# Batch 1's attention in blocks of 64 queries of two heads, batch 0 masked by VectorE with scores on half of TensorE's rows

## The chip, the cores and the metric

One core of a Trainium2 chip. The metric is device time in microseconds. The kernel before ran three times: 541.24, 541.22 and 537.54 us, median 541.22. One further execution was profiled.

## What is computed

The reference takes q, k, v of 4 batches x 8 heads x 576 positions x 64. Heads 0 to 3 are local (a query sees itself and the 31 positions before it), heads 4 to 7 strided (it sees the positions before it of the same class modulo 32). Two blocks of matrix products follow on the 512 channels.

```python
scores = scale * np.matmul(q, k.transpose(0, 1, 3, 2))
mask_local = (rel >= 0) & (rel < stride)                       # stride = 32
mask_strided = (rel >= 0) & (pos[None, :] % stride == pos[:, None] % stride)
attn = softmax(np.where(masks, scores, -1e9)); x = attn @ v    # x: (4, 576, 512)
h = relu(x @ w_in); u, v = split(h); v_n = layernorm(v)
v_s = einsum('ts,bsd->btd', w_spatial, v_n) + b_spatial
x = (u * v_s) @ w_out
theta = x @ w_theta
y = einsum(w_tok_r, x * cos(theta)) + einsum(w_tok_i, x * sin(theta))
u = x + y; out = u + relu(u @ w_ch)
```

## The kernel before, in words

Matrix products are made of pairs of f16 numbers (a high and a low part), three passes each. The weights come as 64-bit floats and are turned into such pairs on the chip, block by block: one ScalarE step (L203), three VectorE steps (L204 to L206), then the high part on ScalarE (L119 for all weights) and the low part on GpSimd (L211). These conversions and the attention of the next batch are woven into the main products of the batch before. A list `conv` has a due time for each block, ATT_AT (L54) a start and a pace in us for each batch's attention, and `others()` (L778) emits whatever is due by a clock that counts matmul columns. Within that, a scheduler fixes the order of instructions on every engine before the program runs; the main path's VectorE, ScalarE and GpSimd operations have a higher priority (`Ahead`, L99; their line in the profile is L108).

The main path of a batch is: v products (L578, main_v), the norm, u and sp products, x products with w_out, th products, and from th by sine and cosine on ScalarE the tile zf, which goes through DMA transposes on SyncE's queue (L686); then y products on zf and c products (main_end). The attention of batch b+1 must be over before main_v(b+1).

Batches 0 and 1 (N32 = 2) do their attention in f32 (attention32, L408), batches 2 and 3 with f16 pairs (attention, L485). The heads are taken in four pairs hp: 0 and 1 local, 2 and 3 strided with the positions sorted by class. For batches 0 and 1, q holds two heads on the two halves of the 128 rows and k comes from memory with zeros: `kzl`, `kzs` have, for head j, the other head's rows zero, so that a matmul over all 128 rows gives one head's scores. A load of k is 608 KB for a local pair and 576 KB for a strided one; the very first pair's is cut in two pieces of 384 and 224 KB (L309). After q and k of a pair comes its v (L318), four or five windows of 128 keys.

A unit is two blocks of a pair (96 queries local, 126 strided, with windows of 128 keys) of both heads, four score blocks of 128 columns; there are 11 units. scores32 (L375) first puts the mask into PSUM by a bf16 matmul of an identity with maskb (L383), then adds four score matmuls (L388). softmax32 (L392) on VectorE takes the maximum of all four blocks (L395) and negates it (L403), and four exponentials on ScalarE (L405) read PSUM and add up the sums. In kind "d" of E_WAY (two units of batch 0) VectorE subtracts (L398), one exponential does all (L400) and VectorE adds up (L401). A step later softmax_div (L340) makes the reciprocals (L341, L342) and multiplies (L343) on VectorE, TensorE transposes (L445), ScalarE copies (L446). Another step later the probabilities are multiplied with v (L420), two heads on two column halves, and x_evac (L345) writes a high part on ScalarE (L355) and a low part on VectorE (L356). The PSUM tile "av" exists once; in batch 1 the transposes use it too.

Batches 2 and 3 load q, k and v through staging tiles qs, ks and vs of their own (L269, L283, L285), convert them (L287 to L290, L295, L296), and mask with a fused VectorE instruction (softmax_exp, L327; L332) that adds the mask, scales by -1/8 and keeps the minimum for each row. Their qT, kT and vT share two slots with q, k and v of batches 0 and 1.

Of the kernel before, what the change touches and what calls it, by code (L numbers as in the profile page):

```python
# [11 lines left out]
F16 = mybir.dt.float16  # L12
BF16 = mybir.dt.bfloat16
F32 = mybir.dt.float32
# [20 lines left out]
E_WAY = ('aaaadaaadaa', 'aaaaaaaaaaa')  # L35
# [4 lines left out]
E_KLO = 'v'  # L40
E_PN16 = 'vvvv'
# [12 lines left out]
ATT_AT = (None, (2.7, 4.0), (74.5, 4.4), (169.9, 4.6))  # L54
# [10 lines left out]
def kernel(  # L65
# [31 lines left out]
    NZ = 2 * S // P  # L97

# [170 lines left out]
    def load_v(b, hp):  # L269
        nb = 6 if hp < 2 else 5  # L270
        vs = att_p.tile([P, 6, 2, 64], F32, tag="vs", name="vs")
        nc.sync.dma_start(vs[:, 0:nb], vl_d[b, hp] if hp < 2 else vs_d[b, hp - 2])
        return vs, nb

    def prep_qk(b, hp, j, tiles):
        local = hp < 2
        nk = S + STRIDE if local else S
        if j == 0:
            qT = att_p.tile([P, 2, S], F16, tag="qT", name="qT", bufs=2)
            kT = att_p.tile([P, 2, 2, S + STRIDE], F16, tag="kT", name="kT", bufs=2)  # L280
# [4 lines left out]
        ks = att_p.tile([P, S + STRIDE], F32, tag="ks", name="ks")  # L285
# [6 lines left out]
    def prep_v(ld):  # L292
        vs, nb = ld
        vT = att_p.tile([P, 2, 6, 2, 64], F16, tag="vT", name="vT", bufs=2)
# [6 lines left out]

    def load32(b, hp):
        local = hp < 2
        nb = 6 if local else 5
        qv = att_p.tile([P, S], F32, tag="qT", name="q32", bufs=2)
        kv = att_p.tile([P, 2, S + STRIDE], F32, tag="kT", name="k32", bufs=2)
        ksrc = kzl[b, hp] if local else kzs[b, hp - 2]
        first = b == 0 and hp == 0
        cuts = (0, 2 * LQ, S) if first else (0, S)  # L309
        for i, (c0, c1) in enumerate(zip(cuts, cuts[1:])):  # L310
            nc.sync.dma_start(qv[:, c0:c1], qp[b, hp][:, c0:c1])
            k0, k1 = (c0 + STRIDE if i else 0, c1 + STRIDE) if local else (c0, c1)
            nc.sync.dma_start(kv[..., k0:k1], ksrc[..., k0:k1])
            if first and i == 0:
                nc.sync.dma_start(mask, mask_d)
                nc.scalar.activation(maskb, mask, AF.Copy)
        vv = att_p.tile([P, 6, 2, 64], F32, tag="vT", name="v32", bufs=2)
        nc.sync.dma_start(vv[:, 0:nb], vl_d[b, hp] if local else vs_d[b, hp - 2])  # L318
        return qv, kv, vv

# [3 lines left out]
    def mask_of(hp, blk):  # L324
        return (1 if blk == 0 else 0) if hp < 2 else (3 if blk == 4 else 2)

    def softmax_exp(u, sc, sm, st):  # L327
        local = units[u][0][0] < 2
        R = LQ if local else P
        for n, (hp, j, blk) in enumerate(blocks_of(u)):  # L330

            nc.vector.tensor_tensor_reduce(out=sm[0:R, n, :], in0=sc[n][0:R], in1=mask[0:R, mask_of(hp, blk), :],  # L332
                                           op0=ALU.add, op1=ALU.min, scale=-0.125, scalar=3e38,
                                           accum_out=st[0:R, 1, n:n + 1])
        for n in range(4):
            nc.scalar.activation(sm[0:R, n, :], sm[0:R, n, :], AF.Exp, bias=st[0:R, 1, n:n + 1],  # L336
                                 scale=-1.0, accum_out=st[0:R, 2, n:n + 1])
# [37 lines left out]
    def scores32(u, tabs, sc, apart):  # L375


        R = LQ if units[u][0][0] < 2 else P
        mi = [mask_of(*un) for un in units[u]]
        for j0, j1 in ((0, 1), (1, 2)) if apart else ((0, 2),):  # L380
            for i0, i1 in [(0, 2)] if mi[0] == mi[1] else [(0, 1), (1, 2)]:
                shape = [P, i1 - i0, j1 - j0, P]
                nc.tensor.matmul(sc[0:R, i0:i1, j0:j1], identb[:, 0:R],  # L383
                                 maskb[:, mi[i0], :].unsqueeze(1).unsqueeze(1).broadcast_to(shape),
                                 start=(i0 == 0), stop=False)
        for n, (hp, j, blk) in enumerate(blocks_of(u)):
            o = LQ * blk if hp < 2 else SOFF[blk]
            nc.tensor.matmul(sc[0:R, n // 2, j], tabs[hp][0][:, o:o + R], tabs[hp][1][:, j, o:o + P],  # L388
                             start=False, stop=(n == 3 or (apart and n == 2)))
        return R  # L390

    def softmax32(sc, sm, st, R, way):  # L392
        X = mybir.AxisListType.X
        mx = st[0:R, 0, :]
        nc.vector.tensor_reduce(out=mx.rearrange("p (i j) -> p i j", i=2), in_=sc[0:R], op=ALU.max, axis=X)  # L395
        smv = sm[0:R].rearrange("p (i j) k -> p i j k", i=2)
        if way == "d":
            nc.vector.tensor_tensor(smv, sc[0:R], mx.rearrange("p (i j) -> p i j", i=2).unsqueeze(3).broadcast_to(  # L398
                [R, 2, 2, P]), ALU.subtract)
            nc.scalar.activation(sm[0:R], sm[0:R], AF.Exp, scale=0.125)  # L400
# [493 lines left out]
```

## Time and profile before

| | us |
|---|---|
| three runs, median | 541.22 |
| profiled execution | 538.83 |
| its span, first to last instruction | 536.8 |
| PE busy | 485.4 (90%) |
| DVE busy | 366.2 (68%) |
| ACT busy | 306.9 (57%) |
| POOL busy | 96.1 (18%) |
| mean granted TensorE clock | 0.977 |

PE is TensorE's matmuls, PEld its weight loads, DVE VectorE, ACT ScalarE, POOL GpSimd, SPq SyncE's DMA queue. An f32 matmul has two records. Durations of neighbouring operations on one engine overlap a little, so an operation's cost in a full queue is the distance from its start to the next one's start.

### The profile page before, as it was taken

To read this page: it belongs to the slowest core of one execution; us is meant where nothing else is said; L and a number is where in the kernel's file an instruction comes from. 1 tells how busy PE (TensorE), PEld (TensorE's weight loads), DVE (VectorE), ACT (ScalarE), POOL (GpSimd) and SP (SyncE) were. 2 spreads that over 40 slices of the span, in tenths; PEclk is the share of its full clock that TensorE was granted. 3 is DMA by queue.
4 is the path that set the end of the run, shared out by engine and by line. 5 is a ranking of instruction groups with operands and counts; after the bars stand their busy time and mean duration, and the time that the engine had idled before them with its cause. 6 is when DMAs were issued, how large, how long until landed. Compare 5 with 4: busy or idle time off the path is not lost. (4 is left out here: it accounts for less than half of the span.)

```text
span 536.8 us, 10338 instructions
## 1 busy us (share of the span) xinstructions
PE 485.4 (90%) x4019; PEld 365.7 (68%) x4019; DVE 366.2 (68%) x817; ACT 306.9 (57%) x737; POOL 96.1 (18%) x72
## 2 busy tenths in 40 slices
PE   6777978777887998999899998999999999996996
PEld 6764556555653776777666876777747777774775
DVE  1788999999987998898558778874389121227212
ACT  1777787667798436777585457764582121158101
POOL 0021134543300542001000400010003300100110
PEclk9789999999898998999999999999999999998999
DMA  8666577454159514755529034522082020004402
GB/s 278 239 232 189 162 262 219 161 152 139 37 98 244 136 40 108 194 135 143 137 40 137 1 81 127 148 45 37 1 150 27 1 89 1 1 2 91 86 1 88
DMA packets 75861, 59.88 MB, mean 112 GB/s; under 512 B 59939, under 2 KB 60963, under 8 KB 75813
## 3 DMA queue, kind: packets, MB, share of 16 engines
q1 hardware_dynamic: 75812, 59.23, 42.2%
q8 instruction: 31, 0.51, 0.4%
q14 instruction: 18, 0.14, 0.1%
HBM read 40.08 MB, written 4.72 MB: 83 GB/s over the span
## 5 line engine op out<-in xcount | busy, mean ns | idle before, releaser
L517 PE MATMUL y<-wtok,zf 128*128 128x288 f16 x864 | 108.8, 288 | 4.1 <-DMA zf<-vn 4.1
L517 PEld LDWEIGHTS <-zf 128*128 128x128 f16 x864 | 84.6, 99 | 27.7 <-DMA zf<-vn 4.7
L517 PE MATMUL sp<-wsp,vn 128*128 128x288 f16 x384 | 50.8, 286 | 2.1 <-ACT vn L108 1.6
L517 PE MATMUL c<-x2h,wch 128*128 128x288 f16 x384 | 49.6, 289 | 1.6 <-ACT o L108 1.6
L517 PE MATMUL x<-zf,wout 128*128 128x288 f16 x384 | 49.7, 288 | 0.0
L517 PE MATMUL th<-x2h,wth 128*128 128x288 f16 x384 | 49.6, 290 | 0.0
L517 PE MATMUL u<-xT,win 128*128 128x288 f16 x384 | 49.5, 286 | 0.0
L517 PEld LDWEIGHTS <-vn 128*128 128x128 f16 x416 | 40.3, 98 | 12.3 <-ACT vn L108 1.8
L578 PE MATMUL v<-win,xT 128*128 128x512 f16 x192 | 44.9, 387 | 3.0 <-DVE xT L356 1.9
L108 POOL TENSOR_TENSOR x2h<-x2f,x2h 128x576 f16<-128x576 f32 x20 | 27.6, 1381 | 110.4 <-DVE x2h L108 42.5
L517 PEld LDWEIGHTS <-wch 128*128 128x128 f16 x384 | 37.8, 99 | 11.7 <-issue 2.0
L517 PEld LDWEIGHTS <-wth 128*128 128x128 f16 x384 | 38.1, 100 | 10.3 <-issue 0.2
L517 PEld LDWEIGHTS <-wout 128*128 128x128 f16 x384 | 37.2, 98 | 9.5
L517 PEld LDWEIGHTS <-win 128*128 128x128 f16 x384 | 37.2, 98 | 9.1
L336 ACT ACTIVATE sm<-sm,st 96x128 f32<-96x128 f32 (+1 forms) x88 | 34.2, 390 | 7.8 <-DVE st L332 7.7
L578 PEld LDWEIGHTS <-xT 128*128 128x128 f16 x192 | 18.8, 99 | 25.3 <-DVE xT L356 2.6
L108 ACT ACTIVATE x2h<-x2f 128x576 f16<-128x576 f32 x24 | 16.5, 686 | 30.4 <-DVE x2f L108 30.0
L108 DVE SCALAR_TENSOR_TENSOR x2f<-y,x2f 128x576 f32<-128x576 f32 x16 | 12.0, 752 | 28.5 <-PE y L517 28.5
L108 POOL TENSOR_TENSOR zf<-u,zf 128x576 f16<-128x576 f32 x8 | 10.3, 1287 | 106.5 <-ACT zf L108 106.5
L108 DVE TENSOR_TENSOR ta<-ta,x2f 128x1152 f32<-128x1152 f32 x16 | 21.5, 1352 | 8.9 <-ACT ta L108 8.9
L108 ACT ACTIVATE o<-c 128x576 f32<-128x576 f32 (+1 forms) x17 | 10.3, 613 | 30.3 <-PE c L517 30.0
L343 DVE TENSOR_TENSOR sm<-sm,st 96x512 f32<-96x512 f32 (+1 forms) x33 | 26.7, 809 | 0.8
(122 smaller groups left out, 890.2 us busy)
## 6 DMA issues: line engine op xcount, KB each, us to landing
qs<-in_qd_dram SPq DMA_DIRECT2D x16, 288.0 KB, 3.0
out_dram<-o SPq DMA_DIRECT2D x15, 288.0 KB, 2.1
x2f<-in_w_in_dram SPq DMA_DIRECT2D x8, 512.0 KB, 5.3
ks<-in_kl_dram SPq DMA_DIRECT2D x8, 304.0 KB, 3.1
k<-in_kzs_dram SPq DMA_DIRECT2D x4, 576.0 KB, 5.4
wstg<-in_w_tr_dram SPq DMA_DIRECT2D x4, 576.0 KB, 4.7
wstg<-in_w_ti_dram SPq DMA_DIRECT2D x4, 576.0 KB, 4.7
ks<-in_ks_dram SPq DMA_DIRECT2D x8, 288.0 KB, 3.2
```

The lines of the kernel that those rows point to most:

```text
L108: return f(*args, **kwargs)
L336: nc.scalar.activation(sm[0:R, n, :], sm[0:R, n, :], AF.Exp, bias=st[0:R, 1, n:n + 1], scale=-1.0, accum_out=st[0:R, 2, n:n + 1])
L343: N[eng].tensor_tensor(sm[0:R], sm[0:R], st[0:R, 3, :].unsqueeze(2).broadcast_to([R, 4, P]), ALU.mult)
L517: nc.tensor.matmul(ps, lhs, rhs, **kw)
L578: nc.tensor.matmul(ps, xh[:, xe, c, i * P:(i + 1) * P], win[:, we, c, DM:2 * DM], start=(c == 0 and n == 0), stop=(c == NC - 1 and n == 2))
```

## The change

Batch 0 (attention0): k is loaded without zeros, each head into its half of the rows, the first pair's k on ScalarE's queue. The four score matmuls of a unit use 64 rows each, head 0 the lower and head 1 the upper half, into different PSUM banks. There is no mask matmul; softmax_exp masks on VectorE as in batches 2 and 3, one instruction a block. One unit (number 8, kind "p") takes the maximum so, subtracts on GpSimd, uses one exponential and adds up on VectorE. The multiplication of softmax_div moves to GpSimd for all 11 units.

Batch 1 (attention1): 12 units. A local unit is three blocks of 64 queries with windows of 96 keys, a strided one four (or three) blocks of 54 queries with 54 keys. Head 0's scores go to PSUM partitions 0 to 63 and head 1's to 64 to 127, each by a matmul over 128 rows with 64 columns of q, so that a unit has 288 or 216 columns on 128 partitions. k's zeros are written once, at the start, by four memsets into kts, and only the nonzero halves are loaded. v is loaded in blocks that begin where the windows begin: 4 DMAs for a local pair, 13 for a strided one, from the same arrays as before. The mask is loaded again in six pieces, and maskb made from it, when batch 1 begins.

Memory: kts (two tiles) and areg are allocated once. v of batches 0 and 1 lies in areg in two regions; over the same columns lie vT of batches 2 and 3 and their staging tiles: vst on columns 1536 to 2303 and qst on 2304 to 2879, the second region of v being 1408 to 2815, while kst lies behind it. identb is made on VectorE instead of GpSimd. Batch 1's pace in ATT_AT goes from 4.0 to 3.85 us a step.

```diff
-E_WAY = ('aaaadaaadaa', 'aaaaaaaaaaa')
+E_SUM = 'aaaaaaaapaa'
+E_PN32 = 'gv'
-ATT_AT = (None, (2.7, 4.0), (74.5, 4.4), (169.9, 4.6))
+ATT_AT = (None, (2.7, 3.85), (74.5, 4.4), (169.9, 4.6))
+    LK, SB, NLB, NSB = 96, 54, 9, 11
...
-    maskb = const.tile([P, 4, P], BF16, name="maskb")
-    nc.gpsimd.tensor_copy(identb, ident)
+    maskb = const.tile([P, 4, LK], BF16, name="maskb")
+    kts = [const.tile([P, 2, S + STRIDE], F32, name=f"kt{i}") for i in range(2)]
+    areg = const.tile([P, 6 * S + STRIDE], F32, name="areg")
+    v32s = [areg[:, i * NSB * P:(i + 1) * NSB * P].rearrange("p (n j d) -> p n j d", n=NSB, j=2) for i in range(2)]
+    vts2 = [areg[:, i * 6 * P:(i + 1) * 6 * P].bitcast(F16).rearrange("p (e n j d) -> p e n j d", e=2, n=6, j=2)
+            for i in range(2)]
+    vst = areg[:, 12 * P:18 * P].rearrange("p (n j d) -> p n j d", n=6, j=2)
+    qst = areg[:, 18 * P:18 * P + S]
+    kst = areg[:, 18 * P + S:18 * P + 2 * S + STRIDE]
+    nc.vector.tensor_copy(identb, ident)
+    for t in kts:
+        nc.vector.memset(t[0:64, 1, :], 0.0)
+        nc.vector.memset(t[64:P, 0, :], 0.0)
...
-        vs = att_p.tile([P, 6, 2, 64], F32, tag="vs", name="vs")
+        vs = vst
...
-            kT = att_p.tile([P, 2, 2, S + STRIDE], F16, tag="kT", name="kT", bufs=2)
+            kT = kts[hp % 2].rearrange("p j n -> p (j n)").bitcast(F16).rearrange("p (e j n) -> p e j n", e=2, j=2)
...
-        qs = att_p.tile([P, S], F32, tag="qs", name="qs")
+        qs = qst
...
+    units32 = [(hp, list(range(3 * u, 3 * u + 3)), LK) for hp in range(2) for u in range(3)]
+    units32 += [(hp, list(range(4 * u, min(4 * u + 4, NSB))), SB) for hp in (2, 3) for u in range(3)]
...
+    def load_kq(qv, kv, b, hp, c0, c1, k0, k1, by=nc.sync):
+        nc.sync.dma_start(qv[:, c0:c1], qp[b, hp][:, c0:c1])
+        ksrc = kzl[b, hp] if hp < 2 else kzs[b, hp - 2]
+        for j in range(2):
+            by.dma_start(kv[64 * j:64 * j + 64, j, k0:k1], ksrc[64 * j:64 * j + 64, j, k0:k1])
...
+    def scores32(u, tab, sc):
...
+        for n0, n1 in zip(cut, cut[1:]):
...
+            nc.tensor.matmul(sc[:, n0:n1, :], identb, maskb[:, mi, 0:W].unsqueeze(1).broadcast_to([P, n1 - n0, W]),
+                             start=(n0 == 0), stop=False)
+        for n, t in enumerate(blks):
+            for j in range(2):
+                nc.tensor.matmul(sc[64 * j:64 * j + 64, n, :], qv[:, q_at(W, t):q_at(W, t) + 64],
+                                 kv[:, j, k_at(W, t):k_at(W, t) + W], start=False, stop=(n == nb - 1))
...
+    def softmax32(u, sc, sm, st):
+        nc.vector.tensor_reduce(out=st[:, 0, 0:nb], in_=sc, op=ALU.max, axis=mybir.AxisListType.X)
+        nc.vector.tensor_scalar(st[:, 1, 0:nb], st[:, 0, 0:nb], -0.125, None, op0=ALU.mult)
+        for n in range(nb):
+            nc.scalar.activation(sm[:, n, :], sc[:, n, :], AF.Exp, bias=st[:, 1, n:n + 1],
+                                 scale=0.125, accum_out=st[:, 2, n:n + 1])
...
+    def pv32(b, u, tab, pT):
...
+            for j in range(2):
+                nc.tensor.matmul(av[64 * j:64 * j + 64, o:o + R], tab[2][0:W, t, j, :],
+                                 pT[0:W, n, 64 * j + r0:64 * j + r0 + R], start=True, stop=True)
...
-    def softmax_exp(u, sc, sm, st):
+    def softmax_exp(u, sc, sm, st, way="a"):
...
+            if way == "p":
+                nc.vector.tensor_tensor_reduce(out=sm[0:R, n, :], in0=sc[n][0:R], in1=mask[0:R, mi, :],
+                                               op0=ALU.add, op1=ALU.max, scale=1.0, scalar=-3e38,
+                                               accum_out=st[0:R, 0, n:n + 1])
...
+        if way == "p":
+            nc.gpsimd.tensor_tensor(sm[0:R], sm[0:R], st[0:R, 0, :].unsqueeze(2).broadcast_to([R, 4, P]), ALU.subtract)
+            nc.scalar.activation(sm[0:R], sm[0:R], AF.Exp, scale=0.125)
+            nc.vector.tensor_reduce(out=st[0:R, 2, :], in_=sm[0:R], op=ALU.add, axis=mybir.AxisListType.X)
...
-                R = scores32(s, tabs, sc, b == 0)
...
+                scs = [two[:, n % 2, n // 2 * P:n // 2 * P + P] for n in range(4)]
...
+                for n, (hp, j, blk) in enumerate(blocks_of(s)):
+                    o = LQ * blk if local else SOFF[blk]
+                    h = slice(64 * j, 64 * j + 64)
+                    nc.tensor.matmul(scs[n][0:R], tabs[hp][0][h, o:o + R], tabs[hp][1][h, j, o:o + P],
+                                     start=True, stop=True)
...
-                softmax_div("v", sm, st, R, XS)
+                softmax_div(E_PN32[b], sm, st, R, XS)
...
-    atts = [(attention32 if b < N32 else attention)(b) for b in range(B)]
+    atts = [attention0(), attention1()] + [attention(b) for b in range(N32, B)]
```

## Rows read from the trace of the kernel before

**Rows 1.** Busy time of each engine in stretches of the span. The columns are the stretch in us, its length, then for PE, PEld, DVE, ACT and POOL the busy time in us with the number of instructions, the granted TensorE clock as a share of 2.4 GHz, the share of the DMA engines' time and GB/s.
```profile
14.00:55.00 41.00, 32.13 (x252) 24.30 (x252) 35.38 (x90) 30.16 (x110) 7.67 (x6) 0.88 0.67 220
55.00:150.00 95.00, 77.97 (x624) 57.50 (x622) 90.77 (x173) 71.14 (x184) 36.67 (x24) 0.98 0.52 162
...
175.00:537.00 362.00, 346.30 (x2981) 264.94 (x2978) 218.15 (x508) 180.52 (x398) 50.77 (x35) 0.99 0.33 76
```

**Rows 2.** What TensorE waited for between 55 and 165 us: engine, tile and line that waited, what released it, then the sum of the waits in us, their number and the longest.
```profile
PE av L445 <- DVE xT L356: 7.7, 5, 3.1
PE av L445 <- DVE sm L343: 5.9, 3, 2.5
```

**Rows 3.** The start: a k load of the first 20 us (count, size, time to landing), the busy times of 10 to 20 us (columns as in rows 1), then the timeline of VectorE and of TensorE: start and duration in us, engine, line, operation, output and inputs, shapes, count, and in brackets the idle time before it and what ended it.
```profile
k<-in_kzl_dram SPq DMA_DIRECT2D x1, 608.0 KB, 6.8
...
10.00:20.00 10.00, 5.57 (x33) 5.38 (x32) 5.07 (x16) 5.03 (x24) 1.15 (x1) 0.71 0.98 356
...
8.42 0.69 DVE L395 TENSOR_REDUCE st<-at 96x4 f32<-96x512 f32 x1 [6.54 <-PE at L388]
14.12 0.43 DVE L204 TENSOR_SCALAR x2h<-x2f 128x512 int32<-128x512 int32 x1 [5.02 <-DMA x2f<-in_w_in_dram]
...
6.03 0.59 PE L383 MATMUL at<-maskb,identb 128*96 128x128 bf16 x4 [1.75 <-ACT maskb L316]
```

**Rows 4.** The timeline of VectorE, columns as in the second part of rows 3: batch 0's softmax steps at 31 to 35 us, and the fused masking and minimum of batch 2 at 200 us.
```profile
31.53 0.15 DVE L403 TENSOR_SCALAR st<-st 128x4 f32<-128x4 f32 x1
31.60 0.15 DVE L341 TENSOR_SCALAR st<-st 96x4 f32<-96x4 f32 x1
...
33.29 0.68 DVE L343 TENSOR_TENSOR smx<-smx,st 96x512 f32<-96x512 f32 x1
33.89 0.68 DVE L395 TENSOR_REDUCE st<-at 128x4 f32<-128x512 f32 x1
34.49 0.34 DVE L356 TENSOR_TENSOR xT<-av,xT 128x192 f16<-128x192 f32 x1
34.76 0.26 DVE L403 TENSOR_SCALAR st<-st 128x4 f32<-128x4 f32 x1
...
200.48 0.28 DVE L332 CUSTOM_DVE_ANT_0 sm<-sc,mask 96x128 f32<-96x128 f32 x1
...
200.68 0.28 DVE L332 CUSTOM_DVE_ANT_0 sm<-sc,mask 96x128 f32<-96x128 f32 x1
```

**Rows 5.** The timelines of GpSimd and VectorE side by side, columns as before: first four VectorE operations of 14 to 55 us that began beside a GpSimd operation, with the first of these GpSimd operations, then three operations at 249 us.
```profile
29.30 1.15 POOL L211 TENSOR_TENSOR win<-x2h,win 128x512 f16<-128x512 f32 x1 [9.95 <-ACT win L119]
...
29.88 1.11 DVE L343 TENSOR_TENSOR smx<-smx,st 96x512 f32<-96x512 f32 x1
...
39.21 1.14 DVE L341 TENSOR_SCALAR st<-st 128x4 f32<-128x4 f32 x1
...
48.66 1.65 DVE L343 TENSOR_TENSOR smx<-smx,st 128x512 f32<-128x512 f32 x1
...
52.83 1.19 DVE L205 SCALAR_TENSOR_TENSOR x2h<-x2f,x2h 128x512 int32<-128x512 int32 x1 [0.98 <-ACT x2f L203]
...
249.52 1.28 POOL L108 TENSOR_TENSOR zf<-u,zf 128x576 f16<-128x576 f32 x1 [2.71 <-ACT zf L108]
...
249.60 0.28 DVE L332 CUSTOM_DVE_ANT_0 sm<-sc,mask 128x128 f32<-128x128 f32 x1
...
250.04 1.37 DVE L288 TENSOR_TENSOR qT<-qs,qT 64x576 f16<-64x576 f32 x1 [0.15 <-ACT qT L119]
```

**Rows 6.** The timeline of TensorE in batch 0's attention and at the first unit of batch 1.
```profile
16.64 1.96 PE L388 MATMUL at<-k,q 128*96 128x128 f32 x8
...
43.80 0.65 PE L420 MATMUL av<-smx,v 128*64 128x126 f32 x8 [0.69 <-ACT smx L446]
44.39 0.39 PE L578 MATMUL v<-win,xT 128*128 128x512 f16 x1
44.61 0.60 PE L445 MATMUL sc<-ident,smx 128*128 128x128 f32 x4
...
52.35 0.42 PE L383 MATMUL sc<-maskb,identb 128*96 128x256 bf16 x2
52.61 1.04 PE L388 MATMUL sc<-k,q 128*96 128x128 f32 x8
53.48 0.59 PE L578 MATMUL v<-win,xT 128*128 128x512 f16 x2
```

**Rows 7.** Batch 2's first q load on SyncE's queue, all its q loads as a group (count, size, median time to landing), the first DMA transposes of zf, and TensorE where batch 1's attention ends and batch 2's begins.
```profile
8.36 0.33 SPq L284 DMA_DIRECT2D qs<-in_qd_dram  x1
...
qs<-in_qd_dram SPq DMA_DIRECT2D x16, 288.0 KB, 3.0
...
154.54 6.43 SPq L686 DMA_TRANSPOSE zf<-vn  x4
...
157.04 0.61 PE L458 MATMUL sc<-kT,qT 128*96 128x128 f16 x8
...
158.41 0.64 PE L420 MATMUL av<-pT,v 128*64 128x126 f32 x8
...
173.38 22.22 PE L517 MATMUL y<-wtok,zf 128*128 128x288 f16 x180
195.44 0.61 PE L458 MATMUL sc<-kT,qT 128*96 128x128 f16 x8
```

More of the change, by code (lines that the diff above doesn't have):

```diff
@@ new lines, in load_kq, with load_v32 @@
+    def load_kq(qv, kv, b, hp, c0, c1, k0, k1, by=nc.sync):
[3 more added lines that the diff above has]
+            by.dma_start(kv[64 * j:64 * j + 64, j, k0:k1], ksrc[64 * j:64 * j + 64, j, k0:k1])
+    def load_v32(vv, b, hp):
+        if hp < 2:
+            src = vl_d[b, hp]
+            nc.sync.dma_start(vv[0:LK, 0:9:3], src[0:LK, 0:6:2])
+            nc.sync.dma_start(vv[0:64, 1:9:3], src[64:P, 0:6:2])
+            nc.sync.dma_start(vv[64:LK, 1:9:3], src[STRIDE:64, 1:6:2])
+            nc.sync.dma_start(vv[0:LK, 2:9:3], src[STRIDE:P, 1:6:2])
+            return
+        src = vs_d[b, hp - 2]
+        for t in range(NSB):
+            p, end = k_at(SB, t), k_at(SB, t) + SB
+            at = p
+            while at < end:
+                w = max(i for i in range(5) if SOFF[i] <= at)
+                w = next((i for i in range(5) if SOFF[i] <= at and SOFF[i] + P >= end), w)
+                n = min(end, SOFF[w] + P) - at
+                nc.sync.dma_start(vv[at - p:at - p + n, t], src[at - SOFF[w]:at - SOFF[w] + n, w])
+                at += n
@@ L312, in load32 @@
             k0, k1 = (c0 + STRIDE if i else 0, c1 + STRIDE) if local else (c0, c1)
[L313 to L318, printed above, removed]
-        return qv, kv, vv
+            load_kq(qv, kv, b, hp, c0, c1, k0, k1, nc.scalar if first else nc.sync)
@@ L373, in spans_of, with attention0 @@
         return spans
[L375 to L400, printed above, removed]
-            nc.vector.tensor_reduce(out=st[0:R, 2, :], in_=sm[0:R], op=ALU.add, axis=X)
-        else:
-            nc.vector.tensor_scalar(st[0:R, 1, :], mx, -0.125, None, op0=ALU.mult)
-            for n in range(4):
-                nc.scalar.activation(sm[0:R, n, :], sc[0:R, n // 2, n % 2, :], AF.Exp, bias=st[0:R, 1, n:n + 1],
-                                     scale=0.125, accum_out=st[0:R, 2, n:n + 1])
-    def attention32(b):
+    def attention0():
+        b = 0
         tabs = {0: load32(b, 0)}
@@ L417, in attention32 @@
                 av = pa("av")
-                for i, hp, blk, r0, rows, o, t0 in pv_blocks(s - 2):
+                for i, hp, blk, r0, R, o, t0 in pv_blocks(s - 2):
                     for j in range(2):
-                        nc.tensor.matmul(av[64 * j:64 * j + 64, o:o + rows], tabs[hp][2][:, blk, j, :],
-                                         pT[:, 2 * i + j, r0:r0 + rows], start=True, stop=True)
+                        nc.tensor.matmul(av[64 * j:64 * j + 64, o:o + R], tabs[hp][2][:, blk, j, :],
+                                         pT[:, 2 * i + j, r0:r0 + R], start=True, stop=True)
                 x_evac(xT[b % 2], spans_of(s - 2), av)
@@ L441, in attention32 @@
                 sm, pT, st, R = un[s - 1]
[L442 to L443 removed]
+                softmax_div(E_PN32[b], sm, st, R, XS)
+                pt = pa4("sc")
                 for n in range(4):
```

135 lines of the change are left out of this document (105 added, 30 removed).

## The prediction, made before the changed kernel was run

> **What bounds the kernel now.** I read the table of busy time by stage first. From 175 us on TensorE is busy for 346.3 of 362 us, so nothing that leaves TensorE's work there alone can gain much [rows 1]. What the change touches lies before that. In the stretch 14 to 55 us VectorE is busy 35.4 of 41 us, ScalarE 30.2, TensorE 32.1 at a granted clock of 0.88. From 55 to 150 us VectorE is busy 90.8 of 95 us and TensorE 78.0 [rows 1]. So I then asked who TensorE waits for between 55 and 165 us: the two longest sums are batch 1's transposes, waiting 7.7 us for the difference of L356 and 5.9 us for the normalization of L343, both on VectorE [rows 2]. VectorE is what sets the pace until batch 1's attention is over. Before 14 us it is the DMA: VectorE does one reduction at 8.42 us and then stands for 5.0 us for the first block of w_in, while the DMA engines are 98% busy in 10 to 20 us [rows 3].
>
> **The start.** Ahead of w_in in the queue stand the k loads of the first two head pairs, 608 KB each with their zeros [rows 3]. Without zeros half of the two, 608 KB, goes. At the 356 GB/s of that stretch [rows 3] they are 622,592 B / 356 GB/s = 1.7 us, by which w_in lands earlier: -1.7 us, from 0 (if something else stands in front of VectorE then) to -2.8 us (at the 220 GB/s of the next stretch, [rows 1]). The first matmul no longer waits 1.75 us for the mask's cast on ScalarE [rows 3]; but VectorE's next work behind unit 0 is w_in either way, so I give that nothing. The four new memsets of 608 columns are about 0.7 us each, by the 0.60 us of a reduction over 512 [rows 4], together 2.8 us; VectorE idles for 6.5 us before 8.42 [rows 3], which hides them. If half of that cover were gone they would still fit.
>
> **Batch 0 on VectorE.** Prices are from start to start, since the ends overlap: a reduction of 512 elements 0.60, a normalization 0.60, the small negation 0.07, the fused mask-add and minimum with its accumulator read 0.20 to 0.21 a block [rows 4]. Before: nine units of 0.60 + 0.07 + 0.60 = 11.4, and two of kind "d" with two reductions, a subtraction and a normalization, 4 x 0.60 = 2.4 each, 4.8: 16.2 us. After: ten units of 4 x 0.21 = 8.4 and one of kind "p" with 0.84 + 0.60 = 1.4: 9.8 us. That is -6.4 us.
>
> Against it stand 12 operations that move to GpSimd (11 normalizations, one subtraction). A GpSimd tensor_tensor over 512 elements takes 1.15 us [rows 5], and VectorE operations that begin beside one are held until it ends: at 29.88 a normalization takes 1.11 instead of 0.68 us, at 39.21 the small L341 1.14 instead of 0.15, at 48.66 a normalization 1.65, at 52.83 a conversion step of the same size 1.19 [rows 4, 5]. The excess is 0.43 + 0.99 + 0.97 + 0.51 = 2.9 us over the six GpSimd operations of 14 to 55 us [rows 1, 5], 0.48 each. The fused reduction, with one operand in PSUM, is not held: at 249.60 it takes its 0.28 us inside a GpSimd operation, and the next VectorE operation, with both operands in SBUF, takes 1.37 [rows 5]. So what can be hit in batch 0 are the steps of w_in's conversion, three a block, and the small L341. I take 12 x 0.48 = 5.8, less the 1.4 us of the two normalizations that are no longer there to be hit: +4.4. Net -2.0 us. Ends: -7.8 us if the new operations hold nobody, and 12 x 1.15 - 7.8 = +6.0 us if each holds VectorE for its whole length. I take the value from the six measured ones.
>
> The Trainium skill ("SBUF — State Buffer", section "Who interferes with whom") speaks against this move: the port pair that VectorE and GpSimd share is an exclusive lock for the whole instruction, and the later one waits. By that rule the upper end, +6.0 us, is as possible as the mean; the sum would be -0.4 instead of -8.4. The trace agrees with the mechanism, not with that size: 0.48 us per operation.
>
> **Batch 0 on TensorE.** The mask matmuls go (0.25 us a unit) and the 0.87 us of scores [rows 6] run on row halves, two heads side by side. Pairs on two column halves show what pairing is worth: eight fp32 probability matmuls of 126 columns take 0.59 us, 74 ns each, against 109 ns for 128 columns unpaired [rows 6]. Up to 11 x (0.25 + 0.28) = 5.8 us; since VectorE is the later one in that stage I count 0. If the pairing gives nothing, 0 too. A loss is possible by the clock (third rival).
>
> **Batch 1.** A unit's reduction and normalization fall from 512 to 288 elements (local) or 216 (strided). Between 192 elements at 0.27 us (L356) and 512 at 0.60 [rows 4], 288 are 0.37 and 216 are 0.29 us. Local: 6 x 2 x 0.23 = 2.8 us. Strided: five units of 1.20 against six of 0.59, 6.0 - 3.5 = 2.5. The twelfth unit brings some 0.3 us of small operations. So -5.0 us of VectorE; at VectorE's share of the stage (0.955) -4.7 us. Ends: -1 us (if the waits of rows 2 only change their releaser) and -5.3. ScalarE's exponentials become 40 narrower ones instead of 44; TensorE has more, shorter matmuls (80 probability ones for 44, paired as before); both have room, 71 and 78 of 95 us [rows 1]. I count 0.
>
> **SyncE.** V in blocks comes in 34 loads instead of 4, k in two pieces, the mask again in 6: some 40 more issues at 0.33 us (the q load of [rows 7]), 13 us of issuing spread over the 110 us in which batch 1 is loaded and worked on. The weights' loads queue behind them, and their conversion stands in VectorE's line anyway; I count 0, at worst +3 us if a quarter of it meets an idle VectorE.
>
> **Batch 2.** Its stages for q and v now overlay the v of batch 1's second and fourth head pair. Today the first q load goes at 8.36 us, long before use; after, they can only go when batch 1's last probability matmul is done, 158.41 us [rows 7]. Behind that: two q loads in turn through one buffer with their conversions. But the third unit's scores come only at 195.44 [rows 7], so there is room to catch up. I count 0; the other end is the second rival.
>
> **Sum.** -1.7 - 2.0 - 4.7 = -8.4 us, against the profiled execution's 538.83 us: 530.4. The middle of the three runs is 541.22, 0.4% above it; from that the same sum gives 532.8. I predict the middle, **531.6 us**, 540.0 - 8.4.
>
> **Rivals.** (A) GpSimd's lock gives batch 0's saving back: -1.7 + 6.0 - 4.7 = -0.4, **539.6 us**. For it: each normalization starts just behind VectorE's reciprocal, so VectorE's next operation meets it at its start, and nearly 1 of 1.15 us was seen twice [rows 5]. Against it: 44 of VectorE's operations then are of the kind that isn't held.
> (B) Slower: the late loads of batch 2. Place: SyncE's queue and TensorE's order around 155 us. The scores of batch 2's unit 0 stand at 157.04 in front of the tail of v(1); if they stay there, TensorE waits for two q loads of 3.0 us [rows 7] with some 1.4 us of conversion each (two steps of the 0.68 us of rows 4), 9 us. A load that waits in SyncE's queue also holds the transposes of zf behind it, which begin at 154.54 and which y at 173.38 needs [rows 7]: 4.5 us if they begin at 159. Together +13.5: -8.4 + 13.5 = +5.1, **545.1 us**. It decides from 8.4 us of hold on. Against it: batch 1 ends earlier, and the static order may move the scores.
> (C) TensorE's clock. With less to do it may be granted the lower level for all of batch 0: the eight records of a unit's scores took 1.96 us at 16.64 against 1.04 at 52.61 [rows 6], nearly the two to one of 1.2 and 2.4 GHz. Work of 32.1 x 0.88 = 28.2 us at full clock, less 2.8 (masks) and half of 11 x 0.87, is 20.6; at half clock 41.2 us, where the forecast leaves 41 - 3.7 = 37.3: +3.9, so -4.5, **535.5 us**. Against it: 0.88 is the mean now.
> The Trainium skill ("TensorEngine Tiling (Array Packing)", section "Key Properties") says a change of tiling mode drains the array; batch 0 would get 22 more. No drain shows at the column-half changes of today: one 512-column matmul between two such groups takes 0.22 us from start to start, its usual spacing [rows 6]. If each cost the 0.17 us by which that matmul's length exceeds its spacing, 3.7 us would be added to TensorE, and C would gain weight.
>
> **How the numbers follow.** Forecast 0.50, A 0.17, B 0.15, C 0.18. A measurement of this kernel tells about 1% (5.4 us) from no change. Below 535.8 lie nine tenths of the forecast, half of C and a little of A: faster 0.56. Above 546.6 lies about half of B and a little of the rest: slower 0.11. Same 0.33. The range from 525 to 543 us takes in the lower ends (-1.7 - 7.8 - 5.3 = -14.8, 525.2), A and C, and leaves out most of B; the forecast's own is 527 to 536.
>
> **What would show it.** Right: first conversion of w_in at about 12.4 us; batch 0's last L356 at 50 instead of 54; VectorE's busy time up to 150 us some 7 us lower although single L205, L206 and L341 last over 1 us beside GpSimd; the y matmuls of batch 0 at 165 instead of 173.4 us; from there on the same distance to the end. Wrong: VectorE as busy as before in 14 to 55 us (A), TensorE idle at batch 2's first scores or late zf transposes (B), a granted clock under 0.75 in 14 to 50 us with TensorE waited for (C), or a later stage that grows.

## The result and the profile after

The changed kernel is slower: 547.1 us median of four runs against 541.2, ratio 1.012 [1.009, 1.016]. The forecast was 531.6 and a range to 543; what came is near rival B's 545.1.

The busy times of the three stretches of [rows 1], in the changed kernel:

```profile
14.00:55.00 41.00, 36.52 (x262) 23.23 (x261) 27.74 (x116) 30.12 (x106) 17.64 (x16) 0.88 0.54 159
55.00:150.00 95.00, 77.85 (x748) 55.74 (x747) 89.06 (x174) 66.04 (x168) 38.64 (x25) 0.93 0.47 152
175.00:537.00 362.00, 344.81 (x2961) 263.28 (x2960) 221.33 (x525) 186.38 (x415) 49.03 (x35) 0.98 0.33 74
```

From 14 to 55 us VectorE is busy 7.6 us less, but this is hardly work saved: before 14 us it is busy 6.5 instead of 1.6 us (the memsets and the first maskings come earlier), and by 55 us it has done 16 instead of 21 steps of w_in's conversion. From 55 to 150 us it is busy 1.7 us less, and TensorE's granted clock is 0.93 where it was 0.98. Behind 175 us TensorE's busy time is 1.5 us lower in the same 362 us: an idle stretch is new there. TensorE's waits from 55 to 205 us, the counterpart of [rows 2], show where:

```profile
PE av L569 <- DVE sm L418: 10.2, 6, 3.0
PE sc L582 <- DVE st L446: 7.6, 1, 7.6
PE av L427 <- ACT pT L570: 2.4, 1, 2.4
...
PE av L569 <- DVE xT L475: 1.6, 2, 1.0
```

One wait of 7.6 us is new. TensorE's timeline has it inside y(0), the y products of batch 0 (batches count from 0; L582 are scores of batch 2, L458 before, and L446 their masking, L332 before):

```profile
173.19 13.40 PE L641 MATMUL y<-wtok,zf 128*128 128x288 f16 x108
186.43 0.61 PE L582 MATMUL sc<-kt,qT 128*96 128x128 f16 x8
186.88 5.55 PE L641 MATMUL y<-wtok,zf 128*128 128x288 f16 x44
200.07 1.01 PE L582 MATMUL sc<-kt,qT 128*96 128x128 f16 x8 [7.63 <-DVE st L446]
200.87 5.69 PE L641 MATMUL y<-wtok,zf 128*128 128x288 f16 x28
```

The reader is to see three things. y(0) starts at 173.19 us, where it started before (173.38, [rows 7]): the lead of 8 us isn't there. The first two units of batch 2, at 157 and 160 us before, now stand inside y(0). And the second unit's scores wait for the one PSUM buffer of scores, which the first unit's masking gives back; the 28 y products behind the wait then take 0.20 us each on average, against 0.127 (the granted clock is 0.50 from 201 to 205 us and 1.00 from 206.4 us on). VectorE's timeline says why the masking is late:

```profile
193.62 1.22 DVE L110 TENSOR_TENSOR vn<-vr,vn 128x1024 f16<-128x1024 f32 x1
194.76 2.34 DVE L218 TENSOR_SCALAR wx<-wstg 128x512 int32<-128x512 int32 x1
197.03 0.28 DVE L446 CUSTOM_DVE_ANT_0 sm<-sc,mask 96x128 f32<-96x128 f32 x1
...
197.23 1.55 DVE L219 SCALAR_TENSOR_TENSOR wx<-wstg,wx 128x512 int32<-128x512 int32 x1
198.71 0.28 DVE L446 CUSTOM_DVE_ANT_0 sm<-sc,mask 96x128 f32<-96x128 f32 x1
```

The scores are there at 187.0; VectorE's fixed order has their four maskings behind batch 1's norm (vn) and between the steps of a weight's conversion. Batch 2's q loads, the counterpart of 8.36 us in [rows 7], went only when batch 1's last PV (161.8 us; PV are the products of the probabilities with v) had freed their staging:

```profile
165.03 0.53 SPq L298 DMA_DIRECT2D areg<-in_qd_dram  x1
...
170.13 0.36 SPq L298 DMA_DIRECT2D areg<-in_qd_dram  x1
```

### The profile page after: what moved, and what is told of

It is laid out like the page before. It is cut to its first block, busy times and chain, and to the rows that moved or that the text cites. A ratio compares the mean times of both kernels' runs of the same rounds, so it can differ in the third digit from the quotient of the medians.

```text
span 546.2 us, 10748 instructions
## 1 busy us (share of the span) xinstructions
PE 490.7 (90%) x4136; PEld 360.3 (66%) x4136; DVE 366.6 (67%) x881; ACT 307.4 (56%) x738; POOL 107.5 (20%) x83
## 5 line engine op out<-in xcount | busy, mean ns | idle before, releaser
L641 PE MATMUL y<-wtok,zf 128*128 128x288 f16 x864 | 112.2, 293 | 3.9 <-DMA zf<-vn 3.9
L641 PEld LDWEIGHTS <-zf 128*128 128x128 f16 x864 | 85.9, 100 | 29.0 <-DMA zf<-vn 4.7
L641 PE MATMUL u<-xT,win 128*128 128x288 f16 x384 | 51.3, 289 | 3.7 <-ACT win L121 2.3
L110 POOL TENSOR_TENSOR x2h<-x2f,x2h 128x576 f16<-128x576 f32 x20 | 26.4, 1320 | 118.2 <-DVE x2h L110 54.5
L702 PE MATMUL v<-win,xT 128*128 128x512 f16 x192 | 46.6, 397 | 0.8 <-ACT xT L474 0.4
L110 DVE TENSOR_TENSOR u<-u,sp 128x576 f32<-128x576 f32 x16 | 12.0, 749 | 21.0 <-PE sp L641 20.8
```

Source lines behind the costliest of these rows:

```text
L110: return f(*args, **kwargs)
L641: nc.tensor.matmul(ps, lhs, rhs, **kw)
L702: nc.tensor.matmul(ps, xh[:, xe, c, i * P:(i + 1) * P], win[:, we, c, DM:2 * DM], start=(c == 0 and n == 0), stop=(c == NC - 1 and n == 2))
```

## The experiments

First all runs in one table: the ratio to the kernel before, with its interval, and from each profile the starts of u(0), th(0), y(0) and th(1). From th(1) to the last matmul all 20 kernels take 265 to 270 us, so most of a difference is there at th(1). Each row is one profiled execution, and some lie a few us from their kernel's median: that of the kernel before 2.4 us below it, b0's 3.1 above, c1's 1.7 below.

| | ratio [95%] | u(0) | th(0) | y(0) | th(1) | y(0) to th(1) |
|---|---|---|---|---|---|---|
| before | 1 | 63.0 | 134.6 | 173.4 | 264.9 | 91.5 |
| after | 1.012 [1.009, 1.016] | 58.6 | 129.9 | 173.2 | 273.7 | 100.5 |
| e1_q_early | 1.007 [1.003, 1.010] | 63.0 | 133.5 | 177.1 | 275.5 | 98.4 |
| e2_before_overlay | 1.008 [1.005, 1.011] | 62.2 | 130.0 | 171.7 | 270.1 | 98.4 |
| e3_start_late | 0.999 [0.996, 1.002] | 58.4 | 130.4 | 174.3 | 269.1 | 94.8 |
| e4_norm_vector | 1.004 [1.001, 1.008] | 66.0 | 136.8 | 170.0 | 270.0 | 100.0 |
| b0_batch0_only | 0.998 [0.995, 1.000] | 60.2 | 126.7 | 168.1 | 267.2 | 99.1 |
| b1_batch1_only | 1.002 [0.999, 1.005] | 65.7 | 137.2 | 169.8 | 268.8 | 99.0 |
| c1_late_vv | 1.002 [0.999, 1.005] | 63.9 | 136.7 | 168.3 | 265.3 | 97.0 |
| e5_busy | 1.018 [1.015, 1.022] | 62.2 | 134.6 | 185.8 | 278.1 | 92.3 |
| e6_mask_ahead | 0.997 [0.994, 1.001] | 61.5 | 134.1 | 178.8 | 273.2 | 94.4 |
| b0_late | 0.996 [0.993, 1.000] | 61.5 | 128.0 | 168.0 | 264.2 | 96.2 |
| b0_ahead | 0.994 [0.991, 0.996] | 58.9 | 125.3 | 166.7 | 263.8 | 97.1 |
| e7_no_warm | 0.999 [0.997, 1.002] | 60.5 | 130.4 | 175.1 | 270.3 | 95.2 |
| e8_tight_ahead | 1.008 [1.004, 1.011] | 61.4 | 135.1 | 172.8 | 275.3 | 102.5 |
| e9_vv_ahead | 1.001 [0.999, 1.003] | 64.1 | 134.9 | 168.1 | 268.6 | 100.6 |
| e10_vv_tight_ahead | 1.001 [0.998, 1.004] | 65.4 | 138.7 | 171.9 | 269.3 | 97.4 |
| e11_vv_qearly_ahead | 1.008 [1.004, 1.011] | 67.6 | 138.0 | 181.1 | 273.3 | 92.2 |
| b0_units_first | 1.000 [0.997, 1.003] | 57.8 | 128.5 | 180.6 | 270.6 | 90.0 |
| full_units_first | 1.005 [1.002, 1.007] | 59.0 | 131.0 | 181.3 | 271.1 | 89.8 |

The profiled executions of e1 (548.6 us, median 543.2) and e6 (546.5, median 539.7) are the longest of their kernels; only waits, order and what the clock did are read from them.

**e1: q's staging moved to where it is free earlier.**

```diff
-    qst = areg[:, 18 * P:18 * P + S]      # over the v of batch 1's fourth head pair
+    qst = areg[:, 6 * P:6 * P + S]        # over that of the third; vst, vT and kst moved to fit
```

> The changed kernel with one thing moved: the buffer into which batch 2's q is loaded lies over the v of batch 1's third head pair, not of its fourth, so that q need not wait for batch 1's last PV (161.8 us). Theory (late staging: that wait makes batch 2's first masking late on VectorE, and TensorE stands 7.6 us in front of y(0)'s last passes, then 2.3 us at half clock): the wait for L446 at 192 to 200 us goes, y(0) ends near 201 instead of 211 us, and the time falls by 8 to 11 us, to 536 to 539 us, 2 to 5 us under the kernel before. Rival (the loss at y(0) comes from VectorE's order and GpSimd's holds, and q's load only happens to be late there): at most 2 us less, 545 to 547 us.

543.2 us, between the two. The first q load now goes at 136.52 us, but the second shares the staging buffer with it and waits for its conversion, and the wait in y(0) is still there:

```profile
136.52 0.33 SPq L298 DMA_DIRECT2D areg<-in_qd_dram  x1
...
163.40 0.43 SPq L298 DMA_DIRECT2D areg<-in_qd_dram  x1
```

```profile
PE sc L582 <- DVE st L446: 8.6, 1, 8.6
```

So an early first load alone does not bring the masking forward in VectorE's order. As the second load is still late, this run does not part the load from the order; e6 below does.

**e2: the overlay alone, on the kernel before.**

```diff
-        qs = att_p.tile([P, S], F32, tag="qs", name="qs")
+        qs = qst                              # over the second region of v of batches 0 and 1
```

> The kernel before with that one part of the change alone: q of batches 2 and 3 is staged over the v of the odd head pairs, which batch 1's last PV (158.4 us) still reads. Nothing else is changed. Late staging: the scores of batch 2's first unit (157 us before) stand in TensorE's order or in VectorE's behind a load that can't start before 159 us; 5 to 10 us more, 546 to 551 us. Rival (batch 2 has room to catch up, as the prediction had it): within 1.5 us of 541.2.

545.6 us, +0.8%, just under the lower end expected. The same wait appears in a kernel that has nothing else of the change:

```profile
PE sc L463 <- DVE st L337: 9.3, 1, 9.3
```

The overlay is thus enough to make the wait; room to catch up there was not.

**e3 and e6: the order alone.** e3 changes due times, e6 VectorE's priorities; buffers and loads stay.

```diff
-ATT_AT = (None, (2.7, 3.85), (74.5, 4.4), (169.9, 4.6))
+ATT_AT = (None, (2.7, 3.85), (86.0, 4.0), (169.9, 4.6))     # e3
```

```diff
+        with tc.high_priority(6000 if u < 2 else 0):              # e6, in att_scores
             softmax_exp(u, [sc[:, n, :] for n in range(4)], sm, st)
```

> The changed kernel with its buffers as they are; only the due times in the plan change, so that batch 2's attention is put into the order 11.5 us later and then in steps of 4.0 instead of 4.4 us (to end at about the same place). Late staging, where what hurts is that TensorE's order has batch 2's second scores ahead of y(0)'s last passes: the scores move out of y(0), the 7.6 us wait goes, and the time falls by 6 to 10 us, to 537 to 541 us. Rival (the lost time is VectorE's own, batch 2's masking has to be done somewhere in this stretch): 545 to 549 us.

> The changed kernel with buffers, loads and due times as they are; batch 2's first two units only get a higher priority for their masking and exponentials, which puts the four maskings of the first unit on VectorE ahead of the last steps of batch 1's norm instead of behind them (some 7 us earlier). Theory (order: the second unit's scores stand in TensorE's order inside y(0), wait there for the one PSUM buffer of scores, which is free only after the first unit's masking, and VectorE's order has that behind batch 1's norm): the wait of 7.6 us goes or falls under 2, and the time by 6 to 9 us, to 538 to 541 us. Rival (the masking only looks late; moving it holds up the norm, and y(0) or c(0) waits for that instead): within 2 us of 547.

540.6 and 539.7 us: both fall as the order theory said, by 1.3 and 1.5% of the changed kernel (from the ratios). In e3 y(0) runs through, in e6 the second unit's scores wait 1.05 us:

```profile
174.32 24.43 PE L641 MATMUL y<-wtok,zf 128*128 128x288 f16 x198
198.58 0.61 PE L582 MATMUL sc<-kt,qT 128*96 128x128 f16 x8
```

```profile
192.03 0.61 PE L582 MATMUL sc<-kt,qT 128*96 128x128 f16 x8
192.48 4.57 PE L642 MATMUL y<-wtok,zf 128*128 128x288 f16 x36
198.10 0.61 PE L582 MATMUL sc<-kt,qT 128*96 128x128 f16 x8 [1.05 <-DVE st L446]
```

In e6 q still comes late and the buffers are the same. The wait at y(0) is a matter of VectorE's order, and it is worth some 7 us. That leaves the change at no difference from before, with 8 us of the forecast still missing.

**b0 and b1: each part alone on the kernel before.** b0 has batch 0's part, with batch 2's staging its own; b1 batch 1's, with e3's late start.

```diff
-    atts = [(attention32 if b < N32 else attention)(b) for b in range(B)]
+    atts = [attention0(), attention32(1)] + [attention(b) for b in range(N32, B)]                        # b0
+    atts = [attention0(), attention1()] + ...      # b1: attention0 here is attention32(0) of before
```

> The kernel before with batch 0's part of the change alone: no mask added on TensorE, the fused masking on VectorE, k loaded and multiplied without zeros, the normalising on GpSimd. Batch 1 is masked on TensorE as before, and the staging buffers of batch 2 stay their own. By the prediction's terms (start -1.7, batch 0 -2.0): 537 to 538 us. Rival, TensorE's clock (seen in the first traces: with fewer matmuls in batch 0 the same 128x96 product takes 0.91 instead of 0.55 us for 10 to 20 us of the stretch from 20 to 42 us; before, for about 5 us): what VectorE gains goes there, 540 to 544 us.

> The kernel before with batch 1's part alone (12 units of 64 queries of two heads, normalised on VectorE), batch 0 as before. Its staging overlays are those of the changed kernel, but batch 2's attention is put into the order late, as in e3, so that the wait at y(0) is not there. By the prediction's term (-4.7 for batch 1): 536 to 537 us. Rival (a twelfth unit makes batch 1 end later, and TensorE's v(1) waits for it at 161 to 165 us, which eats VectorE's gain): 540 to 543 us.

Both rivals came closer than the forecast: 540.2 us (ratio 0.998) and 543.6 (1.002). But both reach y(0) early, by 5.3 and 3.5 us. b0 loses it by the same wait, although its staging is its own; b1 at the start of c(0), on ScalarE's conversion:

```profile
PE sc L524 <- DVE st L350: 8.7, 1, 8.7
```

```profile
PE c L680 <- ACT x2h L110: 5.1, 1, 5.1
```

So the overlay is one way into the wait, and a shift of the fixed order by batch 0's part is another.

**b0_late and b0_ahead: the wait taken from b0** by e3's due times and by e6's priority (diffs as there).

> b0 (batch 0's part alone on the kernel before, all staging buffers its own) with batch 2's attention put into the order late, as in e3. b0's trace reached y(0) at 168.1 us, 5.3 us earlier than the kernel before, and then waited 8.7 us there. If the gain is real and only the wait hides it: 531 to 534 us, faster than both kernels by 1.3 to 2%. Rival (as in b1 and c1, where TensorE did reach c(0) 5 us earlier and the time was still that of before: what comes late then, batch 2's attention, holds c(0) or x(1)): 539 to 542 us.

> b0 with the priority of e6 in place of the late start: the first unit's masking comes on VectorE some 5 us earlier, ahead of the vn steps but still behind the vr steps of batch 1's norm. By the order theory the 8.7 us wait falls to some 3 us: 534 to 536 us. Rival as for e6: 539 to 542 us.

539.3 us, the rival's, and 537.4, between the two. b0_ahead is faster than the kernel before by 0.4 to 0.9% and than the changed one by 1.8%, the best version found. Its wait is down from one of 8.7 us to three of together 3.0:

```profile
PE sc L524 <- DVE st L350: 3.0, 3, 2.0
```

Yet from its lead of 6.7 us at y(0) only 1.1 are left at th(1).

**e4, e5, e7: GpSimd's normalizing, TensorE's rate, the warm-up products.**

```diff
-E_PN32 = 'gv'
+E_PN32 = 'vv'                                 # e4
+                for _ in range(2):            # e5, on e3, ahead of batch 0's transposes
+                    nc.tensor.matmul(pt[:, 0, :], ident, ident, start=True, stop=True)
-WARM = 6
+WARM = 0                                      # e7, on e6
```

> The changed kernel with batch 0's probabilities normalised by VectorE instead of GpSimd (11 instructions of 512 elements, 1.04 us each on GpSimd, about 0.6 us on VectorE). If GpSimd's holds of VectorE cost what the prediction gave them (4.4 us) or more (its rival A): 2 to 5 us less, 542 to 545 us. If they lie beside other work, and the loss sits at y(0) alone: between 1 us less and 4 us more (546 to 551 us), since VectorE gets some 6 us of work back.

> e3 with two more matmuls of 128x128 fp32 (no part of the result) ahead of each of batch 0's 11 groups of transposes, where TensorE waits for the normalised scores: 22 matmuls, 0.24 us each at the full rate, 5.4 us in all. If the half-rate stretch between 22 and 36 us (e3: the 128x96 products at 0.91 us) is due to TensorE's idle gaps and costs time: the products stay at 0.55 us, and the time falls by 1 to 4 us against e3, to 537 to 539.5 us. If the rate does not matter there, or does not react: 540.5 to 544 us, the added work being paid in part.

> e6 without the six warm-up matmuls, which in the changed kernel stand in TensorE's order at 12.8 to 15.7 us, ahead of the first transposes (before: at 1.4 us, with nothing behind them). If they are only in the way: 1.5 to 3 us less than e6. If what they give is the full rate of the products after them (0.91 us down to 0.55 us from 17 us on): 1 to 4 us more than e6.

e4: 543.9 us, some 0.8% under the changed kernel. That is in the range expected for holds of +4.4 us, but it does not price them: VectorE gets the work of 11 normalizations back with it, and c1 and e9 below, which make the same edit where the wait at y(0) is gone, gain nothing by it. e5: 551.3, outside both expectations. The added products did keep the full rate longer (the last fast PV group of 96 columns begins at 29.0 us, in e3 at 20.6), but batch 1's PV in front of v(1) then waited 9.0 us for its transposed scores. They were transposed at 152.09 us; ScalarE's order has their copy behind the sine and cosine of th(0), with three table loads of 1.28 us between:

```profile
168.73 0.57 ACT L572 ACTIVATE pT<-av 54x512 f32<-54x512 f32 x1
```

So e5 settles nothing on what the rate costs. e7: 540.9 against e6's 539.7, no difference beyond the intervals.

**c1, e8, e9, e10: the losses taken away together.** c1 is e3 with e4; e9 is e6 with e4; e8 is e6 with batch 1's steps due every 3.55 us; e10 is e8 with e4.

```diff
-ATT_AT = (None, (2.7, 3.85), ...
+ATT_AT = (None, (2.7, 3.55), ...              # e8, e10
```

> e3 and e4 together: batch 2's attention later in the order, and batch 0 normalised on VectorE. If the two losses are apart (6.6 us at y(0); 3.2 us from GpSimd's holds and its slower normalising): 536.5 to 538.5 us, faster than the kernel before by 0.5 to 0.9%. If both gains are the same microseconds at y(0) (e4 splits the wait there too): 540 to 541 us.

> e6 (the changed kernel without the wait at y(0)) with batch 1's 14 steps due every 3.55 us of the plan instead of 3.85, so that its twelfth unit comes into the order 4.2 us earlier. If the lead that the changed kernel has at th(0) (129.9 us against 134.6 before) is lost because that unit's transposes and PV hold v(1) (158.9 to 165 us, some 3.8 us of idle TensorE there): 2 to 4 us less than e6, 535.5 to 537.5 us. If VectorE sets when batch 1 ends: 539 to 541 us.

> e6 with batch 0 normalised on VectorE instead of GpSimd. In e4 that brought y(0) from 173.2 to 170.0 us, and the wait inside y(0) then hid it. If GpSimd's part is the rest of what is missing: 2 to 4 us less than e6, 535.5 to 537.5 us, faster than the kernel before. If c1's result holds here too (the lead at c(0) is given back later): 539 to 542 us.

> e8 and e9 together. If each takes away a loss of its own: 533 to 535.5 us; if both are the same few us ahead of v(1): as the better of the two.

542.6, 545.5, 541.8 and 543.0 us: none is near its theory, and c1 and e8 are beyond their rivals too. c1 and e9 do reach y(0) at 168 us, 5 us early, and have given 5.5 and 9.1 us back by th(1). My second theory, that the twelfth unit or GpSimd keeps the missing 8 us, fell.

**e11, b0_units_first, full_units_first: batch 2's first units ahead of y(0) again**, as in the kernel before. e11 is e9 with e1's staging; the other two raise the priority of the first conversions and units, on b0 and on the whole change (with e1's staging and e4).

```diff
+        with tc.high_priority(8000):
             prep_qk(b, 0, 0, qk)              # likewise prep_qk(b, 0, 1, qk) and att_scores for s < 2
```

> e9 with q staged over the third head pair's v (as in e1). Here the order has all of batch 2's first two units' scores ahead of y(0), as in the kernel before, so y(0) holds no scores at all. Theory (order): no wait at y(0), 2 to 5 us less than e9, 532 to 536 us. Rival (the scores now stand ahead of batch 1's last PV and of v(1) and wait for q there): 1 to 5 us more than e9.

> b0 (batch 0's part alone, own staging) with a higher priority for batch 2's first conversions and its first two units, so that their scores stand ahead of the rest of v(1) in TensorE's order, as in the kernel before, and their masking ahead of batch 1's norm on VectorE. Theory (order): no wait in y(0), and of b0's lead of 5.3 us at y(0) what is left after these two units' work stays to the end: 533 to 537 us. Rival (nothing is gained but moved: the two units cost ahead of y(0) what they cost behind it): 539 to 542 us, y(0) at 173 us or later.

> The whole change with q staged over the third head pair's v, batch 0 normalised on VectorE, and the same higher priority for batch 2's first conversions and units: in TensorE's order the first two units then stand ahead of and inside th(0), the third ahead of batch 1's last PV. Theory (order): all parts of the change keep their gain, 531 to 536 us. Rival (VectorE, over 90% busy from 55 to 215 us, has to do the same work anyway, and v(1) waits for it as in e11): 540 to 546 us.

545.6, 541.1 and 543.8 us: the rival, three times. y(0) now needs 90 to 92 us to th(1), as before, but starts only at 181 us. In b0_units_first the two units' scores wait themselves, ahead of y(0):

```profile
PE sc L524 <- ACT sm L428: 7.7, 1, 7.7
PE v L586 <- DVE ta L110: 3.2, 1, 3.2
```

Against b0 and e4, y(0) starts 12.5 and 11.3 us later, and from there to th(1) it is 9.1 and 10.2 us less. So the lead that the parts showed at y(0) was in part the work of these units, put off. The kernel before has both units ahead of y(0) as well and starts it at 173.4 us; why it is later here by 7 to 8 us was not tried.

## Why the prediction was wrong

The step that failed is "so there is room to catch up. I count 0" for batch 2, and with it "from there on the same distance to the end". From y(0) to the last matmul it was 369.0 us instead of 359.6, nearly all of the difference between y(0) and th(1). Where the prediction looked at the third unit at 195.44 us, the first two had gone from 157 and 160 us into y(0); their masking shares VectorE with batch 1's norm. Rival B had the cause on its list (late loads of batch 2) and nearly the time, but the wrong place and mechanism: not SyncE's queue and TensorE's order at 155 us, but VectorE's order and the one PSUM buffer at 192 us. The zf transposes were hardly held (153.63 against 154.54, the last at 167.1 against 167.4). So that its 545.1 us came near is luck: the two holds that it adds up did not come.

The second step that failed is the sum in front of it: of the 8.4 us, 4.4 are there at u(0), 4.7 at th(0) and 0.2 at y(0). From th(0) to y(0) it took 43.3 us instead of 38.8. Three things are seen there. Two units' scores of batch 1 come behind th(0), where before it was one. The last unit's transposes wait for the one "av" tile until 158.86 us, though their input is ready at 148.5: ScalarE's order has the evacuation of the unit ahead of it behind the sine and cosine of th(0), and its own copy too:

```profile
156.85 0.33 ACT L474 ACTIVATE xT<-av 128x216 f16<-128x216 f32 x1
```

```profile
158.86 0.51 PE L569 MATMUL av<-ident,sm 128*54 128x128 f32 x3 [0.97 <-DVE xT L475]
161.81 0.86 PE L427 MATMUL av<-pT,areg 54*64 54x54 f32 x12 [2.43 <-ACT pT L570]
```

So batch 1's attention ends 3.4 us later than before (158.41, [rows 7]) and not 8 us earlier. And TensorE's clock is lower: the row from th(0) to y(0) in the changed kernel, then before, then in c1, where the last PV stands at 151.46 us:

```profile
129.89:173.19 43.30, 35.62 (x256) 20.58 (x254) 36.18 (x53) 32.72 (x65) 8.43 (x6) 0.84 0.53 129
```

```profile
134.57:173.38 38.81, 32.22 (x214) 19.44 (x213) 33.57 (x62) 33.61 (x75) 5.49 (x4) 0.92 0.57 121
```

```profile
136.65:168.29 31.64, 28.45 (x224) 17.03 (x221) 26.60 (x37) 26.64 (x52) 6.87 (x5) 1.00 0.47 94
```

In the changed kernel the clock is at 0.50 from 136.9 to 143.7 and from 160.8 to 167.6 us, and TensorE is busy 11.9 us of that; before it is busy 5.3 us at that level. Half the difference, 3.3 us, is an estimate of what the clock takes in this stretch. No run sets the clock or moves that evacuation alone, so how the 4.5 us divide is not shown.

Point by point. The start: k without zeros let the first masking begin at 5.72 instead of 8.42 us, but the first conversion came at 18.36 instead of the forecast 12.4, 4.2 us later than before. The order has six warm-up products, 2.93 us, ahead of the first transposes, and the maskings ahead of w_in:

```profile
12.81 2.93 PE L918 MATMUL av<-ident 128*128 128x128 f32 x12
```

```profile
18.36 0.42 DVE L218 TENSOR_SCALAR x2h<-x2f 128x512 int32<-128x512 int32 x1
```

e7 shows no gain without them. Batch 0: its last evacuation came at 49.79 us (forecast 50), and b0 alone is 5.3 us early at y(0). But VectorE's busy time up to th(1) is 227.0 us in b0 and 224.1 in b0_ahead, against 226.4 before: the forecast 2.0 us less is no more than what the order alone moves. GpSimd's holds were priced too high: VectorE's operations of 14 to 55 us that began beside one last 5.2 us longer than usual in all, against 2.9 before, so 2.3 us more where 4.4 were forecast. For the mechanism, the Trainium skill ("SBUF — State Buffer", "Who interferes with whom") lets the later of two operations that need the port pair shared by VectorE and GpSimd wait until the other ends. The trace agrees: a conversion step of 0.68 us took 1.21 at 31.07 and 1.37 at 35.80, beside GpSimd operations that end at 31.73 and 36.63. Batch 1: VectorE's busy time up to th(1) is 222.0 us in b1 against 226.4 before, 4.3 us less where 5.0 were forecast; a reduction of 288 elements takes 0.36 us from start to start (forecast 0.37), and of the six normalizations of 288 elements in the changed kernel one, beside GpSimd, lasts 1.53 us instead of 0.46. In the whole change that saving is gone too: 226.8 us up to th(1).

The remark on the drain rests on a misread row: the 512-column matmul of [rows 6] stands between a column-half group and transposes on the full array, so it met one such change, not two.

What failed under these terms is their use. I added VectorE's savings of two stages as if the end moved with each. Together they bring no lead to y(0) at all (173.2), apart they bring 5.3 and 3.5; and a lead at y(0) does not carry to th(1), in part because batch 2's first units come with it.

Rival C is partly seen. The 96-column PV groups take 0.55 us at the full rate and 0.91 at half. In the changed kernel they are slow at 29.55 and 33.09 us; in e1, where TensorE's order is the same up to 132 us and VectorE's up to 158, all six are slow, from 17.87 to 36.50:

```profile
24.67 0.55 PE L507 MATMUL av<-smx,areg 128*64 128x96 f32 x8
...
29.55 0.91 PE L507 MATMUL av<-smx,areg 128*64 128x96 f32 x8
```

```profile
21.06 0.91 PE L507 MATMUL av<-smx,areg 128*64 128x96 f32 x8
...
36.50 0.91 PE L507 MATMUL av<-smx,areg 128*64 128x96 f32 x8
```

The first conversion is still level there (18.40 against 18.36 us), but u(0) starts at 63.0 instead of 58.6 us. The rate in batch 0 can thus cost some 4 us, and differ by as much between two executions of the same order; that is seen beside it, not tried by itself. Behind batch 0 the clock is lower than before too: 0.93 against 0.98 from 55 to 150 us, 0.85 against 0.97 from 150 to 205.

What stays open: how the missing 8 us divide between the two displaced units, GpSimd, ScalarE's order at the end of batch 1 and the clock, in batch 0 and behind it. That the clock keeps most of them is a rival that no run excludes. b0_late narrows it for batch 0's part: there the clock is 0.99 from u(0) to th(1) (0.97 before), but 0.78 from 14 us to u(0) (0.90 before). A kernel with both parts, full rate in batch 0 and batch 2's units free of batch 1's norm was not found; a second PSUM buffer for the scores was not tried.

## What to carry to other kernels

When a stage gets faster, look up what else stands in the order beside it: a lead may only be later work put off, and the milestone to price is the first one behind which nothing has moved (here th(1), not y(0)). Before counting a shared staging buffer at nothing, follow its load to the first instruction that is queued in order behind its consumer, on every engine. A one-buffer PSUM tile turns a late instruction on another engine into idle TensorE and then a slow restart (here 7.6 us, and a clock of 0.50 up to 205 us).

## What the runs showed of the hardware

A granted clock of 1.00 in a stretch can mean that the trace has no record of the clock there. From 20 to 40 us the column reads 1.00 in e1, where the PV groups are all slow, and 0.74 in the changed kernel, where two of four are fast:

```profile
20.00:40.00 20.00, 18.88 (x115) 13.90 (x112) 15.06 (x69) 15.14 (x57) 8.56 (x8) 1.00 0.48 148
```

```profile
20.00:40.00 20.00, 16.68 (x112) 11.06 (x113) 17.78 (x76) 16.52 (x60) 11.66 (x11) 0.74 0.63 185
```

The trace of e1 has its first record of the clock at 42.1 us, and there its PV groups of 126 columns go from 0.84 (41.67) to 0.65 us (45.09) without a change in the column. The changed kernel's records begin at 17.4 us and have the clock at 0.50 from 27.7 to 37.9 us, where its two slow groups stand. From the first record on, column and products agree in these two traces; before it, only the durations of a recurring shape tell the level.

The Trainium skill ("TensorE: Matmul & The Clock Gate", Part 1) says that the number of slow products after a start differs between runs of one kernel. The two traces, of two kernels with the same TensorE order up to 132 us, are in line with it: in the changed kernel the first PV group, at 17.65 us, is fast, in e1 all are slow up to 41.67 us.

Scores on two halves of the rows cost less than on the full rows: ten records in 0.83 us from start to start (18.61 to 19.44), 83 ns each against 109 [rows 6]. The column-half products behind them take 0.48 us to the next start (19.44 to 19.92), as they do behind transposes (0.49, 17.65 to 18.14), so no price is seen there for the change of halves.
